# Four neighbouring tokens to a partition: another token order in the load of queries and keys, undone in the copy out of PSUM

## The chip, the cores and the metric

The kernel runs on one core of a Trainium2 chip. The metric is device time in microseconds, the median over runs of the same program. Beside the timed runs one execution was profiled; all rows below come from that one.

## The reference, cut to what matters

Four batch entries, 12 heads, 448 tokens, head size 64. Causal attention is followed by a gated feed-forward part.

```python
scores = (q @ k.transpose(0, 1, 3, 2)) / sqrt(64)         # per batch entry and head, 448 x 448
scores = where(upper triangle, -1e9, scores)
attn   = softmax(scores)                                  # over keys
x      = concat over heads of (attn @ v)                  # 4 x 448 x 768, fp32
h      = relu(x @ w_in); u, v = halves of h               # 768 -> 1024 = 512 + 512
v_n    = layernorm(v) without weights
v_s    = w_spatial @ v_n + b_spatial                      # 448 x 448 over tokens
out    = (u * v_s) @ w_out                                # 512 -> 768
```

The result has to follow the reference with the order of tokens kept everywhere. The change touches the order in which the tokens of `q` and `k` stand on chip before the scores are made.

## The kernel before, in words

The 12 heads of each batch entry are taken two at a time: 24 pairs. The first 10 pairs (`SINGLE`, `TURNED`, together `WIDE`) compute in single precision; the other 14 split every number into two half-precision parts, turn them with transposing transfers, and are not touched by the change.

For a single-precision pair the steps are these. `load` (line 691) issues four transfers on SyncE's queue at line 699: `q` and `k`, two heads each, 112 KB apiece, 40 transfers over the ten pairs. The destination `qk` has 112 partitions; in each lie eight rows of 64 numbers, four chunks of tokens with the two heads side by side. Token `112 c + p` goes to partition `p`, chunk `c`. `qk_turn` (from line 716) makes four TensorE transposes of 112 x 128 for `q` and four for `k` (line 733), each into its 112 columns of one PSUM bank, and copies the bank's 448 columns into the SBUF tile `qkT`: on ScalarE at line 754 or on VectorE at line 756. There are 20 such copies. Then `wide` (line 883) multiplies (matrix products at line 903), takes row maxima on VectorE (928), exponentials on ScalarE (938), scales the rows, transposes them (976), copies them out (1000, 1002) and multiplies by `v` (1208).

Everything is planned ahead: `plan.add` lists some 2,500 operations with an estimated cost, a table `ORDER` sets the sequence in which they are issued, a string `WHERE` sets the engine of those that may run on several. Each engine then works down its own queue in that sequence and waits only where an operand is not there. While the core would otherwise be waiting at the start, TensorE runs short filler products (line 687); how many and where is settled when the program is built. The keys that `plan.add` is given are for the planner; the waits in the program come from the tiles that an instruction reads and writes.

SyncE issues all transfers. A transfer waits for the eighth one before it, since eight semaphores go round.

Of the kernel before, what the change touches and what calls it, by code (L numbers as in the profile page):

```python
# [18 lines left out]
WIDE_PE = 856, 848, 902  # L19
# [278 lines left out]
def kernel(  # L298
# [12 lines left out]
    B, H, S, D = q.shape  # L311
# [4 lines left out]
    CP = 112  # L316
    NU = S // 64
    NCH = S // CP
# [11 lines left out]
    plan = Plan()  # L330
# [10 lines left out]
    def at(buf):  # L341
        return phys[buf.kind][buf.slot]
# [4 lines left out]
    ident = const.tile([128, 128], F32, name="ident")  # L347
# [45 lines left out]
    def q32(t):  # L393
        return t.bitcast(F32)[:, 0:2 * S].rearrange("p (c r) -> p c r", r=128)

    def flat32(t):
        return t.bitcast(F32)[:, 0:S]

    def k32(t):
        return t.bitcast(F32)[:, 2 * S:3 * S]  # L400
# [34 lines left out]
    def c_dve(n, aps=0):  # L435
        return 68 + n / 0.96 + 62 * aps

    def c_act(n, src="S", extra=0):
        return (51 if src == "P" else 93) + n / 1.2 + 93 * extra
# [20 lines left out]
    def const_key(name, sub=0):  # L460
        return ((name,), sub)

    def dma(fn, reads, writes, cost, gate=()):

        plan.add({"SP": cost[0]}, fn, list(reads) + list(gate), writes, move=cost)
# [225 lines left out]
    def load(p):  # L691
        b, i = divmod(p, NP)
        h0 = 2 * i
        s = st[p] = {"qk": Buf("qk")}
        for n, src in enumerate((q, k)):
            if WHOLE[p]:
                for h in range(2):
                    dma(
                        lambda e, n=n, src=src, h=h: nc.sync.dma_start(
                            out=at(s["qk"])[:, n, h:2 * NCH:2], in_=src[b, h0 + h].rearrange("(c p) d -> p c d", p=CP)  # L700
                        ),
                        [], [(s["qk"], (n, h))], LOAD["qk1"],
                    )
                continue
            dma(
                lambda e, n=n, src=src: nc.sync.dma_start(
                    out=at(s["qk"])[:, n], in_=src[b, h0:h0 + 2].rearrange("h (c p) d -> p (h c) d", p=CP)
                ),
                [], [(s["qk"], n)], LOAD["qk2"],
            )  # L710
# [3 lines left out]
    def qk_turn(p):  # L714

        s = st[p]
        t = s["qkT"] = Buf("qkT")
        if not WIDE[p]:

            def clear(e):  # L720

                if not blank.get(at(t).name):
                    nc.gpsimd.memset(q32(at(t)), 0.0)
                    blank[at(t).name] = True

            plan.add({"POOL": 819}, clear, [], [(t, (0, 0)), (t, (0, 1))])
        for n in range(2):
            pt = Buf("ps")

            def turn(e, n=n, pt=pt):  # L730
                src = at(s["qk"])[:, n].rearrange("p (c h) d -> p c (h d)", h=2)
                for c in range(NCH):
                    nc.tensor.transpose(
                        out=at(pt)[:, CP * c:CP * c + CP], in_=src[:, c], identity=ident[:CP, :CP]
                    )

            plan.add(
                {"PE": 386}, turn, [(s["qk"], (n, 0)), (s["qk"], (n, 1)), const_key("ident")],
                [(pt, 0), (t, "room")], cls="T",
            )  # L740
            parts = [(slice(0, 64), 0), (slice(64, 128), 64)] if n == 0 and not WIDE[p] else [(slice(0, 128), None)]
            for i, (rows, c0) in enumerate(parts):

                def copy(e, pt=pt, rows=rows, c0=c0, n=n):
                    src = at(pt)[rows, :S]
                    if c0 is None:
                        dst = k32(at(t)) if n else flat32(at(t))
                        if not n:
                            blank[at(t).name] = False
                    else:  # L750
                        dst = q32(at(t))[rows, :, c0:c0 + 64]
                        src = src.rearrange("p (c r) -> p c r", r=64)
                    if e == "ACT":
                        nc.scalar.activation(out=dst, in_=src, func=AF.Copy)
                    else:
                        nc.vector.tensor_copy(out=dst, in_=src)

                plan.add({"ACT": c_act(S, "P"), "DVE": c_dve(S)}, copy, [(pt, 0)], [(t, (n, i))])
        s["qkT_keys"] = [(t, (0, 0)), (t, (1, 0))] + ([] if WIDE[p] else [(t, (0, 1))])

    def qk_prepare(p):
        if WHOLE[p]:
            qk_turn(p)
            return
# [129 lines left out]
    def wide(p, eb, et):  # L894


        s = st[p]
        banks = [Buf("ps") for _ in GROUPS]
# [9 lines left out]
        def both(g):  # L908
            for i in range(len(GROUPS[g])):
                for h in range(2):  # L910
                    _, q0, n, o0, _ = GROUPS[g + h][i]
                    product(h, q0, n, banks[g + h], o0, 0, 128)

        def last():
            for h in range(2):
                product(h, 384, S, banks[4], 0, 64 * h, 64)
# [2 lines left out]
        whose = [(sums[g // 2], 2 * (g % 2) if g < 2 else g % 2) for g in range(5)]  # L919
        for n, fn in enumerate((lambda e: both(0), lambda e: both(2), lambda e: last())):  # L920
            parts = [(banks[g], u) for g in (2 * n, 2 * n + 1) if g < 5 for u in range(len(GROUPS[g]))]
            plan.add({"PE": WIDE_PE[n]}, fn, s["qkT_keys"], parts + [(eb, "room")], tail=70, cls="R")
        for g, (ps, group) in enumerate(zip(banks, GROUPS)):
            sm, u0 = whose[g]
            for u, (h, q0, n, o0, _) in enumerate(group):
                plan.add(
                    {"DVE": c_dve(n) + 40},
                    lambda e, ps=ps, n=n, u=u0 + u, sm=sm, o0=o0, h=h: nc.vector.tensor_tensor_reduce(  # L928
                        out=at(ps)[:, o0:o0 + n], in0=at(ps)[:, o0:o0 + n],
                        in1=mask[:, 0:n] if h is None else mask2[:, 512 - n:512],  # L930
                        scale=-0.125, scalar=3.0e38, op0=ALU.add, op1=ALU.min, accum_out=at(sm)[:, u:u + 1],
                    ),
                    [const_key("mask" if h is None else "mask2")], [(ps, u), (ps, "t"), (sm, f"m{u0 + u}")], tail=138,
                )
            for u, (_, _, n, o0, c) in enumerate(group):
                plan.add(
                    {"ACT": c_act(n, "P", 2)},
                    lambda e, ps=ps, n=n, u=u0 + u, sm=sm, o0=o0, c=c: nc.scalar.activation(  # L938
                        out=at(eb)[:, 128 * c:128 * c + n], in_=at(ps)[:, o0:o0 + n], func=AF.Exp, scale=-1.0,
                        bias=at(sm)[:, u:u + 1], accum_out=at(sm)[:, 4 + 2 * u:5 + 2 * u],  # L940
                    ),
                    [(sm, f"m{u0 + v}") for v in range(len(group))], [(ps, u), (sm, f"s{u0 + u}"), (eb, c)],
                )
        for n, sm in enumerate(sums):
            m = (4, 2, 1)[n]
            plan.add(
                {"DVE": 70},
                lambda e, m=m, sm=sm: nc.vector.tensor_reduce(
                    out=at(sm)[:, 12:12 + m], in_=at(sm)[:, 4:4 + 2 * m].rearrange("p (u t) -> p u t", t=2),
                    axis=AX.X, op=ALU.add,  # L950
                ),
# [4 lines left out]
                lambda e, m=m, sm=sm: nc.vector.reciprocal(out=at(sm)[:, 12:12 + m], in_=at(sm)[:, 12:12 + m]),  # L956
                [], [(sm, "d")],
            )
        for g, group in enumerate(GROUPS):
            sm, u0 = whose[g]  # L960
# [22 lines left out]
            for i in range(2 if g < 2 else 1):  # L983
# [20 lines left out]
                n = (256, 128)[i] if g < 2 else 128 * cn  # L1004
                plan.add({"ACT": c_act(n, "P"), "DVE": c_dve(n)}, copy, [(pt, 0)], [(et, (g, i))])

    def attend(p):
# [22 lines left out]
        if WIDE[p]:  # L1030
            wide(p, eb, et)
# [404 lines left out]
    tail = [None]  # L1436
# [217 lines left out]

    constants()
    load(0)
    qk_prepare(0)
    prep_in(0)
    load(1)
    v_load(0)  # L1660
    v_prepare(0)
    for p in range(NPAIR):
        if p + 2 < NPAIR:
            load(p + 2)
        if p + 1 < NPAIR:
            if (p + 1) % NP == 0:
                v_load((p + 1) // NP)
            qk_prepare(p + 1)
            v_prepare(p + 1)
        attend(p)  # L1670
        if p == 1:
            prep_in(1)
        if p == 3:
            prep_sp()
        if p == 4:
            prep_out([const_key("wst", 0), const_key("wst", 1)])
        if p % NP == NP - 1:
            ffn(p // NP)
# [35 lines left out]
```

## Time and profile before

| | |
|---|---|
| median of 3 runs | 363.12 us (361.66 to 364.56) |
| the profiled execution's own time | 362.61 us |
| its span, first to last instruction | 360.9 us |
| TensorE busy | 346.5 us, 96% |
| VectorE busy | 281.5 us, 78% |
| ScalarE busy | 267.7 us, 74% |
| transfers | 160,588 packets, 56.18 MB; 154,849 packets under 512 B |

The profiled execution stands 0.51 us under the median. Its span leaves 1.71 us for what lies before the first and behind the last instruction. Busy shares are averages over the whole; attention in single precision lies in the first 110 us, where the three compute engines are loaded otherwise than later.

### The profile page before, as it was taken

Reading aid. Unit: us, or ns where it says so; the run is one execution under the profiler, and the core shown is the slowest. Engines: PE = TensorE matmul, PEld = TensorE weight load, DVE = VectorE, ACT = ScalarE, POOL = GpSimd, SP = SyncE. Lnnn points to the kernel's source line nnn. Section 1 sums busy time; section 2 is a strip of 40 time slices with the busy share of each in tenths; the row PEclk is TensorE's granted clock in tenths of the full one; section 3 lists DMA queues with packets and bytes.
Section 4 is the critical chain, followed back from the end, with each engine's and each line's share of the span. In section 5 each row is a group of like instructions: output and inputs, shape, how many; then the busy total and the mean of one; then the engine's idle time right before and its main releaser. Section 6 shows DMA issues by size and latency. Waiting matters only on the chain. (4 is left out here: it accounts for less than half of the span.)

```text
span 360.9 us, 8078 instructions
## 1 busy us (share of the span) xinstructions
PE 346.5 (96%) x2603; PEld 223.8 (62%) x2603; DVE 281.5 (78%) x1103; ACT 267.7 (74%) x768; POOL 165.4 (46%) x230
## 2 busy tenths in 40 slices
PE   6999999999999898999999999999999999999995
PEld 4576575455555545765555679754765896454694
DVE  4998897998999899877986997887979976242421
ACT  2889999899999898888799887659788774222101
POOL 3421645157654657442467775525576500035400
PEclk9999999999999999999999999999999999999999
DMA  7978988855877899878999998887919978300023
GB/s 167 219 185 220 229 178 202 190 132 123 189 171 174 189 225 174 171 161 169 177 172 214 189 182 188 182 165 129 174 36 175 189 138 160 109 2 0 3 87 88
DMA packets 160588, 56.18 MB, mean 156 GB/s; under 512 B 154849, under 2 KB 156322, under 8 KB 160546
## 3 DMA queue, kind: packets, MB, share of 16 engines
q1 hardware_dynamic: 160546, 55.68, 75.1%
q8 instruction: 20, 0.33, 0.4%
q14 instruction: 22, 0.18, 0.2%
HBM read 26.76 MB, written 5.51 MB: 89 GB/s over the span
## 5 line engine op out<-in xcount | busy, mean ns | idle before, releaser
L1426 PE MATMUL pf<-wi,xT 128*128 128x512 f16 (+1 forms) x360 | 62.5, 338 | 0.0
L1426 PE MATMUL pf<-xT,wi 128*128 128x448 f16 x288 | 60.3, 353 | 0.0
L1426 PE MATMUL pf<-wo,g 128*128 128x384 f32 x288 | 54.8, 341 | 0.0
L1079 ACT ACTIVATE ps<-ps,sm 128x256 f32<-128x256 f32 (+4 forms) x98 | 45.4, 464 | 9.6 <-DVE sm L1067 7.7
L1168 DVE SCALAR_TENSOR_TENSOR e<-ps,sm,e 128x384 f16<-128x384 f32 (+4 forms) x98 | 46.1, 505 | 6.4 <-ACT e L487 6.0
L1426 PEld LDWEIGHTS pf<-wo,g 128*128 128x128 f32 x288 | 49.7, 188 | 1.8 <-issue 1.2
L1067 DVE CUSTOM_DVE_ANT_0 ps<-ps,mask,sc 128x256 f32<-128x256 f32 (+4 forms) x98 | 46.7, 505 | 1.8 <-PE ps L1057 1.1
L487 ACT ACTIVATE e<-ps,sm 128x384 f16<-128x384 f32 (+4 forms) x98 | 44.0, 507 | 3.9 <-DVE sm L1101 1.9
L489 POOL TENSOR_SCALAR e<-e,sm 128x384 f32<-128x384 f32 (+3 forms) x39 | 23.1, 600 | 46.5 <-DVE sm L956 30.4
L1426 PEld LDWEIGHTS <-xT 128*128 128x128 f16 (+1 forms) x360 | 26.7, 103 | 27.3 <-issue 7.5
L1426 PEld LDWEIGHTS <-wi 128*128 128x128 f16 x288 | 27.2, 99 | 26.4 <-issue 3.3
L1426 PE MATMUL pf<-wst,vn 128*128 128x448 f16 (+1 forms) x176 | 36.9, 353 | 0.4 <-ACT u L1571 0.3
L938 ACT ACTIVATE e<-ps,sm 128x128 f32<-128x128 f32 (+3 forms) x70 | 34.4, 507 | 3.2 <-DVE sm L928 2.6
L903 PE MATMUL ps<-qkT 64*128 64x128 f32 (+3 forms) x160 | 27.8, 450 | 0.6 <-ACT wi L487 0.3
L1426 PEld LDWEIGHTS <-vn 128*128 128x128 f16 (+1 forms) x176 | 16.7, 98 | 16.6 <-issue 1.3
L976 PE MATMUL ps<-ident,e 128*128 128x128 f32 x160 | 24.4, 279 | 2.3 <-DVE e L1168 1.2
L928 DVE CUSTOM_DVE_ANT_0 ps<-ps,e 128x128 f32<-128x128 f32 (+2 forms) x60 | 24.3, 441 | 2.6 <-PE ps L903 2.5
L1516 POOL TENSOR_TENSOR ln<-ln,mhalf 128x1 f32<-128x1 f32 (+1 forms) x16 | 9.0, 562 | 37.8 <-DVE ln L1508 35.9
L1057 PE MATMUL ps<-qkT 128*64 128x256 f16 (+4 forms) x196 | 26.0, 284 | 0.0
L1056 PE MATMUL ps<-qkT 128*64 128x256 f16 (+4 forms) x196 | 24.4, 290 | 1.1 <-DVE e L1168 0.6
L489 POOL TENSOR_SCALAR qk<-qk,sc 112x512 f32<-112x512 f32 x17 | 13.2, 778 | 26.6 <-DVE sc L543 11.0
L976 PEld LDWEIGHTS ps<-ident,e 128*128 128x128 f32 x160 | 17.9, 142 | 9.7 <-POOL e L489 2.1
(165 smaller groups left out, 737.3 us busy)
## 6 DMA issues: line engine op xcount, KB each, us to landing
wb<-in_moe_w_in_dram SPq DMA_DIRECT2D x12, 512.0 KB, 5.6
vnat<-in_v_dram SPq DMA_DIRECT2D x24, 192.0 KB, 4.6
out_dram<-o SPq DMA_DIRECT2D x12, 384.0 KB, 3.3
qk<-in_k_dram SPq DMA_DIRECT2D x14, 224.0 KB, 3.8
qk<-in_q_dram SPq DMA_DIRECT2D x14, 224.0 KB, 4.0
o<-in_moe_w_out_dram SPq DMA_DIRECT2D x8, 384.0 KB, 3.4
qk<-in_q_dram SPq DMA_DIRECT2D x20, 112.0 KB, 5.4
qk<-in_k_dram SPq DMA_DIRECT2D x20, 112.0 KB, 4.7
```

Source lines behind the costliest of these rows:

```text
L487: nc.scalar.activation(out=dst, in_=src, func=AF.Copy, scale=scale)
L489: nc.gpsimd.tensor_scalar(out=dst, in0=src, scalar1=scale, scalar2=1.0, op0=ALU.mult, op1=ALU.mult)
L903: nc.tensor.matmul(out=at(bank)[r0:r0 + rn, o0:o0 + n], lhsT=flat32(t)[rows, q0:q0 + rn], rhs=k32(t)[rows, :n], start=True, stop=True, ski ...
L928: lambda e, ps=ps, n=n, u=u0 + u, sm=sm, o0=o0, h=h: nc.vector.tensor_tensor_reduce(out=at(ps)[:, o0:o0 + n], in0=at(ps)[:, o0:o0 + n], in ...
L938: lambda e, ps=ps, n=n, u=u0 + u, sm=sm, o0=o0, c=c: nc.scalar.activation(out=at(eb)[:, 128 * c:128 * c + n], in_=at(ps)[:, o0:o0 + n], fu ...
L976: nc.tensor.transpose(out=at(pt)[:, 128 * i:128 * i + 128], in_=e32(at(eb))[:, c0 + i, :], identity=ident)
L1056: nc.tensor.matmul(out=o, lhsT=w, rhs=qkT[:, 2 + x, :n], start=True, stop=False)
L1057: nc.tensor.matmul(out=o, lhsT=w, rhs=qkT[:, 4 + x, :n], start=False, stop=True)
L1067: lambda e, ps=ps, n=n, u=u, sm=sm, o0=o0, m0=m0: nc.vector.tensor_tensor_reduce(out=at(ps)[:, o0:o0 + n], in0=at(ps)[:, o0:o0 + n], in1=m ...
L1079: nc.scalar.activation(out=dst, in_=src, func=AF.Exp, scale=-1.0, bias=at(sm)[:, u:u + 1], accum_out=at(sm)[:, 4 + 2 * u:5 + 2 * u],)
L1168: lambda e, part=part, src=src, sm=sm, u=u: nc.vector.scalar_tensor_tensor(out=part(1), in0=src(), scalar=at(sm)[:, 12 + u:13 + u], in1=pa ...
L1426: nc.tensor.matmul(out=o, lhsT=a(), rhs=rhs, start=(n0 + n == 0), stop=(n0 + n == len(mms) - 1), skip_group_check=len(out_ap()) > 1,)
```

## The change

A token is put elsewhere in the load and put back in the copy. With the new pattern partition `p` gets the tokens `4 p` to `4 p + 3`, so that a partition's four rows of a head are 1 KB in one piece in memory. In the destination they are still four rows of 256 B, 512 B apart, since the other head's rows lie between. After the transposes, column `112 c + p` of the bank holds token `4 p + c`. The copy reads the bank in that sequence and writes with a step of four numbers (16 B), as 4 runs of 112, so that `qkT` has the tokens in their old order. Nothing after the copy changes.

```diff
@@ load
-  out=at(s["qk"])[:, n, h:2 * NCH:2], in_=src[b, h0 + h].rearrange("(c p) d -> p c d", p=CP)
+  out=at(s["qk"])[:, n, h:2 * NCH:2], in_=src[b, h0 + h].rearrange("(p c) d -> p c d", p=CP)
@@ qk_turn
-  {"PE": 386}, turn, [(s["qk"], (n, 0)), (s["qk"], (n, 1)), const_key("ident")],
+  {"PE": 386}, turn, [(s["qk"], (n, 0)), (s["qk"], (n, 1)), const_key("ident"), const_key("banks")],
@@ qk_turn, copy
-  dst = k32(at(t)) if n else flat32(at(t))
+  dst = (k32(at(t)) if n else flat32(at(t)))[:, 0:S].rearrange("p (r c) -> p c r", c=NCH)
+  src = src.rearrange("p (c r) -> p c r", c=NCH)
@@ wide
-  plan.add({"PE": WIDE_PE[n]}, fn, s["qkT_keys"], parts + [(eb, "room")], tail=70, cls="R")
+  plan.add({"PE": WIDE_PE[n]}, fn, s["qkT_keys"] + [const_key("banks")], parts + [(eb, "room")], tail=70, cls="R")
@@ wide, exponentials
-  [(sm, f"m{u0 + v}") for v in range(len(group))], [(ps, u), (sm, f"s{u0 + u}"), (eb, c)],
+  [(sm, f"m{u0 + v}") for v in range(len(group))] + [const_key("small"), const_key("pads")],
+  [(ps, u), (sm, f"s{u0 + u}"), (eb, c)],
```

The added keys (`banks`, `small`, `pads`) name cells that are set once at the start; they alter the planner's list of dependences. In the built program every engine's sequence, its waits and the filler products are what they were. What differs is the form of the 20 copies and the source pattern of the 40 loads, which is built as 448 rows of 64 where it was 112 x 4 x 64, while the destination stays 112 x 4 x 64. The 40 loads also lose a mark in the built program (`ant_dge_precooked`) that they, the loads of weights and the 128-row loads of `v` carry before, and that the 64-row transfers (line 814, part of line 1649) never had.

In VectorE's queue, at the first copy (`qkT_84` is the turned tile, `ps_72` the bank; the rows around it are cells set to constants):

```order
 L663 MEMSET vnat_88 64x6x64
-L756 COPY qkT_84<-ps_72 128x448
+L757 COPY qkT_84<-ps_72 128x4x112
 L679 MEMSET vn_66 64x256
 L680 MEMSET vn_66 1x512
 L681 MEMSET vn_66 1x512
```

The copy stands at the same place with another shape; the line number is one higher because of the added line.

## Rows read from the trace of the kernel before

**Rows 1.** The page: busy us, share of the span and instructions of each engine.

```profile
PE 346.5 (96%) x2603; PEld 223.8 (62%) x2603; DVE 281.5 (78%) x1103; ACT 267.7 (74%) x768; POOL 165.4 (46%) x230
```

**Rows 2.** Busy time by stretches: stretch, length, engines (instructions), granted clock, DMA share, GB/s.

```profile
0.00:3.80 3.80, 1.04 (x5) 0.47 (x5) 1.79 (x16) 1.28 (x1) 2.88 (x18) 1.00 0.39 89
3.80:10.00 6.20, 6.20 (x37) 4.36 (x37) 3.38 (x12) 1.67 (x5) 0.38 (x5) 1.00 1.01 228
10.00:20.00 10.00, 9.86 (x74) 6.13 (x70) 9.14 (x40) 9.04 (x33) 5.06 (x10) 1.00 1.04 188
20.00:40.00 20.00, 19.32 (x171) 12.78 (x170) 18.51 (x72) 17.68 (x57) 3.96 (x6) 1.00 0.88 223
40.00:60.00 20.00, 19.68 (x147) 12.00 (x147) 18.54 (x65) 19.70 (x61) 13.31 (x17) 1.00 0.95 201
60.00:72.00 12.00, 11.14 (x86) 6.32 (x81) 10.44 (x38) 10.47 (x33) 1.77 (x3) 1.00 0.76 181
72.00:90.00 18.00, 17.57 (x130) 10.52 (x129) 16.71 (x70) 17.63 (x49) 10.93 (x17) 1.00 0.56 131
90.00:110.00 20.00, 19.93 (x145) 10.34 (x143) 19.45 (x84) 19.85 (x58) 11.56 (x15) 1.00 0.76 166
```

**Rows 3.** Timeline of SyncE's queue, first loads: start, us, instruction, count.

```profile
0.79 0.94 SPq L699 DMA_DIRECT2D qk<-in_q_dram  x2
1.77 1.02 SPq L699 DMA_DIRECT2D qk<-in_k_dram  x2
```

**Rows 4.** Line 699 in the first 6 us: from issue to landing.

```profile
DMA to landing us min/median/max: 2.3/2.9/5.4
```

**Rows 5.** Timeline of TensorE, first pair: transposes (L733), score products (L903).

```profile
3.79 0.98 PE L733 MATMUL ps<-ident,qk 112*128 112x112 f32 x4 [1.65 <-POOL e L648]
...
5.24 0.98 PE L733 MATMUL ps<-ident,qk 112*128 112x112 f32 x4
...
6.86 1.37 PE L903 MATMUL ps<-qkT 64*128 64x128 f32 x8
```

**Rows 6.** Timeline of ScalarE: the first copies and the exponential behind them.

```profile
6.26 0.54 ACT L754 ACTIVATE qkT<-ps 128x448 f32<-128x448 f32 x1 [3.64 <-PE ps L733]
8.80 0.54 ACT L754 ACTIVATE qkT<-ps 128x448 f32<-128x448 f32 x1 [2.00 <-DVE sm L928]
9.42 0.37 ACT L938 ACTIVATE e<-ps,sm 128x128 f32<-128x128 f32 x1
```

**Rows 7.** Timeline of SyncE's queue: two unmarked 64-row transfers in a row.

```profile
278.72 1.23 SPq L1649 DMA_DIRECT2D out_dram<-o  x2
```

**Rows 8.** Groups by form: copies out of PSUM on VectorE and ScalarE, count, busy, mean ns.

```profile
L756 DVE COPY qkT<-ps 128x448 f32<-128x448 f32 x9 | 5.5, 616 | 2.6 <-PE ps L733 2.5
L1002 DVE COPY et<-ps 128x128 f32<-128x128 f32 x4 | 1.1, 282 | 0.0
L1002 DVE COPY et<-ps 128x512 f32<-128x512 f32 x1 | 0.7, 680 | 0.0
L754 ACT ACTIVATE qkT<-ps 128x448 f32<-128x448 f32 x11 | 5.9, 549 | 6.2 <-PE ps L733 4.2 <-DVE sm L928 2.0
L1000 ACT ACTIVATE et<-ps 128x512 f32<-128x512 f32 x9 | 5.6, 626 | 0.0
L1000 ACT ACTIVATE et<-ps 128x128 f32<-128x128 f32 x16 | 4.4, 283 | 1.9 <-DVE et L1002 1.8
```

**Rows 9.** Groups by form: a read that takes every second word, and GpSimd's subtraction.

```profile
L1243 DVE TENSOR_SCALAR wa<-wb 128x512 int32<-128x512 int32 x12 | 5.1, 421 | 2.4 <-DMA wb<-in_moe_w_in_dram 2.4
...
L521 POOL TENSOR_TENSOR qks<-qk,qks 112x512 f16<-112x512 f32 x19 | 22.1, 1169 | 3.7 <-DVE qks L485 1.6 <-ACT qks L487 1.5
```

**Rows 10.** Busy time by stretches, with queries and keys only, and with weights among them.

```profile
4.00:5.00 1.00, 1.00 (x7) 0.83 (x6) 0.19 (x1) 0.00 (x0) 0.18 (x3) 1.00 0.98 221
...
8.00:9.00 1.00, 1.00 (x12) 0.81 (x9) 0.55 (x3) 0.20 (x1) 0.00 (x0) 1.00 0.96 287
```

**Rows 11.** The page: packets of all transfers.

```profile
DMA packets 160588, 56.18 MB, mean 156 GB/s; under 512 B 154849, under 2 KB 156322, under 8 KB 160546
```

## The prediction, made before the changed kernel was run

> **What bounds the kernel now.** I begin with the page's busy shares: TensorE is busy 346.5 us of 360.9 [rows 1], more than any other engine. An average does not say what holds it in the part where the change acts, so the second view is busy time by stretches over the first 110 us [rows 2], with all 40 loads and all 20 copies in it. Up to 3.8 us TensorE works 1.04 us; from 3.8 to 10 it is busy throughout, though with the filler products, which are work for show. From 10 to 110 us it idles 2.5 us in all (the stretches' lengths less the busy column, 6 rows), VectorE 7.2 us and ScalarE 5.6 us. So three engines run at 93 to 98% side by side: there is little room for more work on VectorE or ScalarE, but what room there is lies on them and not on TensorE. The granted clock is 1.00 in all of these stretches.
>
> The third view is the timeline of the first 10 us, which is a chain. SyncE issues two loads of `q` in 0.94 us and two of `k` in 1.02 us [rows 3]; a load lands 2.3 to 5.4 us after its issue, 2.9 in the median [rows 4]. TensorE's transposes of `q` start at 3.79 us, those of `k` at 5.24 us, and the first scores at 6.86 us [rows 5]. The fourth load is issued at about 1.77 + 1.02 / 2 = 2.28 us; with the median landing that gives 5.2 us, where the transposes of `k` start. Their copy on ScalarE runs from 6.26 to 6.80 us [rows 6], and the scores follow 0.06 us later. Load four, the transposes, the copy of `k`: none of them has cover at the start. What grows here moves everything that comes after, since the engines behind it are nearly full.
>
> **The loads: issuing.** Same count, same place, same bytes. The 40 issues lose their mark in the built program. No row shows a load of this form without it. The nearest rows are the unmarked 64-row stores: two in a row take 1.23 us [rows 7], against 1.02 us for two marked loads [rows 3]. That is 0.105 us more for each. Lower bound nothing, if the difference belongs to stores; upper bound the whole 0.21 us for each issue, if all of it belonged to one of the two. I take 0.105. At the start four issues lie before the landing of load four: 4 x 0.105 = 0.42 us on the path (0 to 0.84). Behind them the other 36 issues, 3.8 us over 70 us of queue, are covered by the transfers themselves: the 16 DMA engines are busy 1.01 and 1.04 from 3.8 to 20 us [rows 2], and SyncE waits for them. If that cover were gone, a load would be late by some tenths, and tiles of later pairs are asked for ahead of use.
>
> **The loads: moving.** The source is now one piece of 1 KB for a partition, the destination still four runs of 256 B. Most packets are under 512 B already (154,849 of 160,588) [rows 11]; 40 x 448 = 17,920 of them are these loads, if each row is a packet. I take it that a packet stays what the shorter side makes it, 256 B, and that nothing is won: the destination, which I know, has not changed. The other end: with 4 KB weight rows among the traffic the engines moved 287 GB/s in a microsecond where they moved 221 with queries and keys alone [rows 10]. At those rates 112 KB (114,688 B) takes 0.40 us instead of 0.52 us, 0.12 us for each load, 4 x 0.12 = 0.5 us at the start.
>
> [...]
>
> **The copies.** Twenty of them, 9 on VectorE at 616 ns and 11 on ScalarE at 549 ns [rows 8]. Fixed part and part per column come from the neighbouring copies: VectorE (680 - 282) / 384 = 1.04 ns a column, ScalarE (626 - 283) / 384 = 0.89 ns. For 448 columns that is 0.46 and 0.40 us. The reading side is as before, in sequence; the writing side steps 16 B. No row has such a step. The nearest one is VectorE taking every second word, a step of 8 B: 512 of them in 421 ns [rows 9], faster than the contiguous copy of 512 (680 ns). So a step by itself costs nothing there, and the lower end is 0. For the upper end I take the slowest elementwise work in the trace, GpSimd's subtraction at 1169 / 512 = 2.28 ns a column [rows 9]: 448 x (2.28 - 1.04) = 0.56 us more on VectorE, 448 x (2.28 - 0.89) = 0.62 us on ScalarE. I take 0, since the row with a step on the same engine is nearer in kind than another engine's, though it reads and has half the step; the size of the doubt is in the chances.
>
> **Other edits.** The added keys are the planner's alone; sequence, waits and fillers are as before, so they cost nothing and need no cover.
>
> **The sum.** 0.42 us from issuing, 0 from moving, 0 from the copies. Against the profiled execution's own 362.61 us this gives 363.0. That execution stands 0.51 us under the median, 363.12; on the median's scale the forecast is 363.5 us, no change that can be told.
>
> **Rivals.**
>
> *A, the copies get slower by about one column time per column, and it comes through.* Place: each of the 20 copies, with the engine's next instruction right behind it, as the exponential at 9.42 us behind the copy from 8.80 to 9.34 [rows 6]. Price 0.46 us on VectorE, 0.40 on ScalarE. Three of ScalarE's copies lie in the first 12 us (at 6.26, 8.80 and 11.02), where nothing takes it up: 1.2 us. The other 8 on ScalarE add 3.2 us, the 9 on VectorE 4.1 us. If idle time takes them up (5.6 and 7.2 us from 10 to 110 [rows 2]), the time is 363.12 + 0.42 + 1.2 = 364.7 us; if ScalarE's come through whole, 363.12 + 0.42 + 11 x 0.40 = 367.9 us, which is slower. The point that decides: over 1% needs 3.6 - 0.42 = 3.2 us from 11 copies, so 0.29 us on each, with full passage. For it: engines at 93 to 98%. Against it: the step of 8 B that costs nothing, and the idle time.
>
> [...]
>
> *B, the loads move faster.* 0.12 us for each load, so that 0.5 us at the start outweighs the issuing, and VectorE's 2.4 us of waiting for weights (last column of line 1243 [rows 9]) shrinks as the transfer queues empty sooner. Time 363.12 - 0.1 to 363.12 + 0.42 - 0.5 - 2.4, thus 360.6 to 363.0 us. Against it: the destination's runs of 256 B, and that TensorE idles so little from 10 us on.
>
> *C, the change does not do what it says:* the packets remain 256 B and 160,588 in number, and the loads gain nothing. That is part of my forecast, so it needs no other price.
>
> **Chances and range.** Forecast 0.47. A over the 1% bound 0.22; A taken up in part, 364.7 to 366.7 us, 0.16. B 0.10. A start that is worse than counted or something else 0.05. About 1%, 3.6 us, is what a measurement of this kernel can tell from no change. Faster by over 1%, below 359.5: only the far end of B with something unseen, 0.06. Slower by over 1%, above 366.8: 0.24. Within: 0.70. The range goes from 361.0 (most of B inside) to 368.0 (A at full passage); about 1 in 10 lies above it and a little less below. The forecast's own range is 362.5 to 364.7, with issuing from 0 to 0.84 us and a few tenths between runs.
>
> **What would show it.** Right: the copies stay near 616 and 549 ns; packets stay near 160,588; two first loads of `k` take about 1.23 us to issue; the first scores start near 7.3 us; after that TensorE idles as before. Rival A: copies near 1.08 and 0.95 us, with idle time of TensorE before the scores (line 903) and transposes (976) up to 90 us. Rival B: fewer or shorter packets and a DMA share well under 1 from 3.8 to 20 us, with the landing under 2.9 us. I am wrong altogether if TensorE's idle time from 10 to 110 us moves by more than 3 us with copies and loads unchanged, as then something that I have called equal is not.

## The result, and the profile after

| | median | runs | lowest to highest |
|---|---|---|---|
| before | 362.40 us | 6 | 361.35 to 364.56 |
| after | 367.62 us | 6 | 365.86 to 369.15 |

The ratio is 1.0133, with an interval of 1.0100 to 1.0166: slower by 4.8 us (3.6 to 6.0). The forecast, 363.5 us, was 4.1 us too low; the time lies inside the range, at its upper end, and inside what rival A gave (364.7 to 367.9 us). The profiled execution of after took 367.97 us, with a span of 366.2.

The page of after, in the order of [rows 1] and [rows 11]:

```profile
PE 349.6 (95%) x2603; PEld 225.4 (62%) x2603; DVE 284.4 (78%) x1103; ACT 271.4 (74%) x768; POOL 164.9 (45%) x230
...
DMA packets 160588, 56.18 MB, mean 153 GB/s; under 512 B 154849, under 2 KB 156322, under 8 KB 160546
```

Instructions and packets are the same to the last one. VectorE is busy 2.9 us more, ScalarE 3.7 us.

The groups by form that answer to [rows 8] (count, busy us, mean ns of one, idle before them):

```profile
L757 DVE COPY qkT<-ps 128x448 f32<-128x448 f32 x9 | 8.8, 976 | 3.6 <-PE ps L733 3.5
L755 ACT ACTIVATE qkT<-ps 128x448 f32<-128x448 f32 x11 | 10.8, 1002 | 7.8 <-PE ps L733 7.8
L1002 ACT ACTIVATE et<-ps 128x512 f32<-128x512 f32 x9 | 5.7, 631 | 0.0
```

That is the extra work. A copy takes 976 ns on VectorE instead of 616 and 1002 ns on ScalarE instead of 549: 360 and 453 ns more, 0.80 and 1.01 ns for each of 448 columns. The neighbouring copy without a step (631 ns, 626 before) has not changed. In all it is 9 x 0.360 + 11 x 0.453 = 3.2 + 5.0 = 8.2 us of engine time, against 4.8 us in the run time. Two engines share it and run side by side, so the sum is not a time on one path. (The page's busy times grow by less, 6.6 us in all: they count instructions that overlap once, and some of ScalarE's others came out shorter.)

The start, by the timeline. SyncE, which answers to [rows 3]; TensorE, to [rows 5]; ScalarE, to [rows 6] (start, us, instruction, count, idle before it; `...` stands for rows left out):

```profile
0.79 1.41 SPq L699 DMA_DIRECT2D qk<-in_q_dram  x2
2.24 1.29 SPq L699 DMA_DIRECT2D qk<-in_k_dram  x2
```

```profile
4.77 0.98 PE L733 MATMUL ps<-ident,qk 112*128 112x112 f32 x4 [2.62 <-DMA qk<-in_q_dram]
...
6.18 0.95 PE L733 MATMUL ps<-ident,qk 112*128 112x112 f32 x4
...
8.18 1.65 PE L904 MATMUL ps<-qkT 64*128 64x128 f32 x8 [0.41 <-ACT qkT L755]
```

```profile
7.17 0.96 ACT L755 ACTIVATE qkT<-ps 128x448 f32<-128x448 f32 x1 [4.55 <-PE ps L733]
...
10.81 0.97 ACT L755 ACTIVATE qkT<-ps 128x448 f32<-128x448 f32 x1 [2.68 <-PE ps L733]
11.57 0.34 ACT L939 ACTIVATE e<-ps,sm 128x128 f32<-128x128 f32 x1
```

Read from top to bottom: four issues end at 3.53 us instead of 2.79, the transposes start 0.98 us later, the copy of `k` lasts 0.96 us instead of 0.54, and the scores start at 8.18 us instead of 6.86, now with a wait of 0.41 us for that copy. The wait is the copy's growth (0.42 us): here nothing covers it. ScalarE's second copy starts at 10.81 us instead of 8.80, so the lag is 2.0 us by then.

More than the wait comes on top. The same two groups of TensorE's instructions, seven filler products and the next scores, first before, then after:

```profile
8.60 0.93 PE L687 MATMUL pf<-ones 128*128 128x256 f16 x7
9.46 0.92 PE L903 MATMUL ps<-qkT 64*128 64x384 f32 x4
```

```profile
10.56 1.59 PE L687 MATMUL pf<-ones 128*128 128x256 f16 x7
12.09 0.92 PE L904 MATMUL ps<-qkT 64*128 64x384 f32 x4
```

From the first scores to these it is 2.60 us before (6.86 to 9.46) and 3.91 us after (8.18 to 12.09), for the same instructions and with no wait in either. TensorE works at about half of its later pace up to a point that comes later in after: in both traces the transposes start 187 ns apart early on and 96 ns apart later, and the change lies where the trace's record of the granted clock has its first entry, 1.00, at 7.82 us before and at 11.91 us after. Before, TensorE had worked without a pause from 3.79 us up to there; after, from 4.77 us, with the pause of 0.41 us for the copy in between. So the lag of 2.6 us at the second row is 0.9 us of a later start, 0.4 us of waiting and 1.3 us of slower pace. How long the slow pace lasts can be told in all traces of this document (one for each kernel) from the 41 filler products (line 687), which are the same in all: they take 331 to 334 ns on average in the four with slow copies in the first pair (after, `copies_only`, `early_only`, `step_32`), and 308 ns in seven of the nine others, 313 in `step_8` and 320 in `pe_side` (the runs follow below). In the first three of the four the scores wait 0.41 us for the copy. The slow copies and the late change of pace go together, but that the one makes the other is not shown.

Busy time by stretches, to be laid beside [rows 2]:

```profile
3.80:10.00 6.20, 4.83 (x23) 3.47 (x24) 2.19 (x4) 0.96 (x1) 0.38 (x5) 1.00 0.81 191
10.00:20.00 10.00, 9.87 (x60) 5.65 (x60) 7.97 (x39) 7.99 (x29) 3.32 (x7) 1.00 1.15 213
20.00:40.00 20.00, 19.40 (x168) 13.45 (x167) 18.85 (x69) 18.38 (x57) 3.32 (x7) 1.00 0.70 186
40.00:60.00 20.00, 19.12 (x144) 11.44 (x141) 18.40 (x62) 19.18 (x54) 11.64 (x16) 1.00 0.97 201
60.00:72.00 12.00, 11.99 (x85) 6.72 (x85) 11.27 (x40) 11.97 (x40) 4.63 (x6) 1.00 0.76 208
72.00:90.00 18.00, 17.44 (x135) 10.55 (x132) 16.62 (x62) 17.20 (x47) 8.87 (x14) 1.00 0.66 147
90.00:110.00 20.00, 19.68 (x143) 10.72 (x142) 19.37 (x88) 19.83 (x57) 12.36 (x18) 1.00 0.69 146
```

From 10 to 110 us TensorE is idle 2.5 us, VectorE 7.5 and ScalarE 5.4 us; before it was 2.5, 7.2 and 5.6. The sums are nearly the same, but they are not made of the same waits. VectorE's 2.4 us of waiting for weights (line 1243 in [rows 9]) are gone, and so is a wait of TensorE for GpSimd (the one for GpSimd is gone in the trace of `late_only` too, and is there in those of `loads_only`, 1.1 us, and `reversed`, 1.0 us); waits for the slow copies stand there instead. TensorE's wait before (us in total, times, longest), then after VectorE's group by form and TensorE's waits:

```profile
PE ps L976 <- POOL e L489: 0.9, 1, 0.9
```

```profile
L1245 DVE TENSOR_SCALAR wa<-wb 128x512 int32<-128x512 int32 x12 | 5.0, 421 | 0.0
PE ps L904 <- DVE qkT L757: 0.5, 1, 0.5
PE ps L978 <- DVE qkT L757: 0.3, 1, 0.3
```

By stretches, TensorE's idle time falls from 0.86 to 0.01 us between 60 and 72 us and grows from 0.32 to 0.88 us between 40 and 60. So idle time takes up a part of the growth, and the copies make about as much anew. How much is taken up in the median is open, since these waits move from trace to trace: `step_8` (below), with copies almost as before, waits for weights 0.3 us. The lag shows it too. ScalarE's copies on either side of 60 to 71 us, first before, then after:

```profile
59.64 0.57 ACT L754 ACTIVATE qkT<-ps 128x448 f32<-128x448 f32 x1
71.66 0.98 ACT L754 ACTIVATE qkT<-ps 128x448 f32<-128x448 f32 x2
```

```profile
64.13 1.06 ACT L755 ACTIVATE qkT<-ps 128x448 f32<-128x448 f32 x1
75.22 1.81 ACT L755 ACTIVATE qkT<-ps 128x448 f32<-128x448 f32 x2 [0.23 <-PE ps L733]
```

The lag is 4.5 us at the first and 3.6 us at the second. The clock column says 1.00 in every stretch, as before; ahead of the record's first entry that says nothing. The last copy on VectorE starts at 89.6 us instead of 85.2 (first rows of the views below; duration min/median/max, then first and last start).

```profile
L756 DVE COPY qkT<-ps x9: 593/615/625, 4.8 to 85.2; 128x448 f32<-128x448 f32 x9
```

```profile
L757 DVE COPY qkT<-ps x9: 943/980/1000, 5.8 to 89.6; 128x448 f32<-128x448 f32 x9
```

The first row is before, the second after. The lag grows from 1.0 to 4.4 us, though not evenly. On TensorE 1.4 us of it is idle time from 3.8 to 10 us (4.83 us busy instead of 6.20). TensorE also counts 3.1 us more of busy time over the run (349.6 against 346.5) for the same 2,603 instructions; the 1.3 us of slower pace stand there. The largest share of the 3.1 us is in the score products, the same 160 in both, with 27.8 us before (first fence) and 29.2 us after.

```profile
L903 PE MATMUL ps<-qkT 64*128 64x128 f32 (+3 forms) x160 | 27.8, 450 | 0.6 <-ACT wi L487 0.3 <-ACT e L938 0.2
```

```profile
L904 PE MATMUL ps<-qkT 64*128 64x128 f32 (+3 forms) x160 | 29.2, 457 | 1.3 <-DVE qkT L757 0.5 <-ACT qkT L755 0.4 <-ACT e L939 0.2
```

New among the releasers are the two copies, 0.9 us together, both before the score products.

### The profile page after: what moved, and what is told of

The parts are those of the page before. It is cut to its first block, busy times and chain, and to the rows that moved or that the text cites. A ratio compares the mean times of both kernels' runs of the same rounds, so it can differ in the third digit from the quotient of the medians.

```text
span 366.2 us, 8078 instructions
## 1 busy us (share of the span) xinstructions
PE 349.6 (95%) x2603; PEld 225.4 (62%) x2603; DVE 284.4 (78%) x1103; ACT 271.4 (74%) x768; POOL 164.9 (45%) x230
## 2 busy tenths in 40 slices
DMA packets 160588, 56.18 MB, mean 153 GB/s; under 512 B 154849, under 2 KB 156322, under 8 KB 160546
## 5 line engine op out<-in xcount | busy, mean ns | idle before, releaser
L904 PE MATMUL ps<-qkT 64*128 64x128 f32 (+3 forms) x160 | 29.2, 457 | 1.3 <-DVE qkT L757 0.5
```

The source lines that it names most:

```text
L904: nc.tensor.matmul(out=at(bank)[r0:r0 + rn, o0:o0 + n], lhsT=flat32(t)[rows, q0:q0 + rn], rhs=k32(t)[rows, :n], start=True, stop=True, ski ...
```

## The experiments

Three theories stood against each other at first. Theory C, the copies: the growth of all 20 copies makes the time, about equally wherever they stand. Theory S, the start: what counts is what happens before the first scores, issues and first copies; later growth is taken up. Theory Q, the queue: the 36 later loads are issued late too, and tiles arrive late. Then two more questions came: what in the copy costs, and whether the loads could gain anything. All differences in us are the ratio less 1, times the median of before in the same comparison, with the ends of the ratio's interval in brackets.

### Each part alone: `loads_only` and `copies_only`

```diff
@@ loads_only: before, with the new load
-  in_=src[b, h0 + h].rearrange("(c p) d -> p c d", p=CP)
+  in_=src[b, h0 + h].rearrange("(p c) d -> p c d", p=CP)
@@ copies_only: before, with the new copy
-  dst = k32(at(t)) if n else flat32(at(t))
+  dst = (k32(at(t)) if n else flat32(at(t)))[:, 0:S].rearrange("p (r c) -> p c r", c=NCH)
+  src = src.rearrange("p (c r) -> p c r", c=NCH)
```

> The load of four neighbouring tokens alone; the copy out of PSUM is contiguous as before, so the tokens of the ten single-precision pairs stay permuted (the part of the computation that is changed). Theory S (start chain): the loss comes from a late start (fourth load 0.9 us later, first copies 0.4 us longer each) and is passed on whole, while what comes after 14 us is taken up by idle time. Then this alone costs 0.9 to 1.5 us: 363.3 to 363.9 us beside 362.4, first scores near 7.8 us instead of 6.86. Theory C (every copy counts): the loads cost nothing that lasts, 362.4 +- 0.4. Theory Q (the queue of loads: 36 later issues are longer too, and tiles arrive late): 365 to 366.

> The copy with a step of 16 B alone; loads as before, so the tokens are put in a wrong order (the part that is changed). Theory S: 2.5 to 3.5 us more than before, 365 to 366 us, nearly all of it by 25 us on the chip's clock; copies near 0.98 us on VectorE and 1.00 us on ScalarE as in the changed kernel. Theory C: all 11 copies of ScalarE come through, 11 x 0.45 = 5.0 us, 367.4 us, the lag growing evenly up to 86 us. Theory Q: 1 to 1.5 us more, 363.4 to 363.9 us.

`loads_only`: median 362.55 us against 362.49, ratio 1.0002 (0.9976 to 1.0029): +0.1 us (-0.9 to 1.1). `copies_only`: 367.82 us, ratio 1.0156 (1.0112 to 1.0201): +5.7 us (4.1 to 7.3). The groups by form of `copies_only`:

```profile
L757 DVE COPY qkT<-ps 128x448 f32<-128x448 f32 x9 | 8.8, 974 | 2.8 <-PE ps L733 2.7
L755 ACT ACTIVATE qkT<-ps 128x448 f32<-128x448 f32 x11 | 10.8, 1002 | 7.1 <-PE ps L733 7.1
```

The copies alone give the whole slowdown, with 974 and 1002 ns, as in after. Theory C's 5.0 us for them holds; theory S's 2.5 to 3.5 us lies below the interval, and theory Q's 1 to 1.5 us far below it. The loads alone give nothing that can be told, though their issues are as slow as in after (1.41 and 1.29 us for two), so theory S's share for the loads is refuted in its upper part, and theory Q's 365 to 366 us altogether.

### The mark on the loads: `unmarked`

```diff
@@ load: before, with the 40 loads issued without their mark
+  nc.dge_precook = False
   nc.sync.dma_start(...)
+  nc.dge_precook = True
```

> The kernel before with the mark taken from its 40 single-precision loads; token order, copies and everything else as before. If the mark is all that the loads cost (theory S), this is the same as the kernel with the new load alone within 0.5 us, two issues take near 1.29 us instead of 1.02, and the fourth load lands near 5.5 us instead of 4.96. If the contiguous source gains something of its own, this is slower than the new load alone by 0.5 us or more; if it costs something, faster by as much.

Median 363.47 us, ratio 1.0043 (1.0014 to 1.0072): +1.6 us (0.5 to 2.6). Timeline of SyncE in this run:

```profile
0.80 1.43 SPq L701 DMA_DIRECT2D qk<-in_q_dram  x2
2.26 1.30 SPq L701 DMA_DIRECT2D qk<-in_k_dram  x2
```

So the longer issue comes from the lost mark and not from the order of tokens. As to its worth, this run and `loads_only` agree only where their intervals overlap, at 0.5 to 1.1 us. Its median is 0.9 us above that of `loads_only`, more than the 0.5 us that was allowed if the mark were all; a gain from the contiguous source would look like this, but `reversed` (below) has that source with the mark kept and shows none.

### Where a slower copy comes through: `early_only` and `late_only`

```diff
@@ qk_turn, copy: before, with the new copy in some pairs
+  if p < 2:        # early_only; in late_only: if p > 1
+      dst = dst[:, 0:S].rearrange("p (r c) -> p c r", c=NCH)
+      src = src.rearrange("p (c r) -> p c r", c=NCH)
```

> The counterpart: the step of 16 B for the pairs 0 and 1 alone, 4 copies before 12 us (wrong token order there, the part that is changed). Theory S: 2 us or more, by the lag of 2.2 us that the kernel with all copies stepped has at 12 us. Theory C: 4/20 of the whole, 0.8 to 1.5 us. The sum with the kernel of late copies should give the 4.0 to 7.3 us of all twenty.

> Loads as before; the copy with a step of 16 B for the pairs 2 to 9 alone, 16 copies from 17 us on (their tokens are put in a wrong order, the part that is changed). Theory S (only the copies at the start come through, later ones are taken up by idle time): 0 to 1 us more than before. Theory C (every copy counts alike): 16/20 of the 4.0 to 7.3 us that all twenty cost, 3.2 to 5.8 us.

The copies by form, of `early_only` and then of `late_only` (the means mix slow and unchanged copies):

```profile
L757 ACT ACTIVATE qkT<-ps 128x448 f32<-128x448 f32 x11 | 7.2, 663 | 8.9 <-PE ps L733 8.9
L759 DVE COPY qkT<-ps 128x448 f32<-128x448 f32 x9 | 5.9, 653 | 3.6 <-PE ps L733 3.6
```

```profile
L757 ACT ACTIVATE qkT<-ps 128x448 f32<-128x448 f32 x11 | 9.5, 885 | 5.6 <-PE ps L733 4.0 <-DVE sm L931 1.6
L759 DVE COPY qkT<-ps 128x448 f32<-128x448 f32 x9 | 8.5, 944 | 2.8 <-PE ps L733 2.7
```

| | growth of the copies | time | interval |
|---|---|---|---|
| `early_only` | 11 x 114 + 9 x 37 ns = 1.6 us | 364.22, +2.4 us | 1.4 to 3.3 |
| `late_only` | 11 x 336 + 9 x 328 ns = 6.6 us | 365.09, +3.3 us | 2.3 to 4.3 |
| `copies_only` | 11 x 453 + 9 x 358 ns = 8.2 us | 367.82, +5.7 us | 4.1 to 7.3 |

The two parts add up to the whole, in growth and in time. The growth in the first two pairs comes through in full (1.6 us lies in the interval), of the growth in the other eight about half does (2.3 to 4.3 of 6.6). Theory S falls on `late_only`, for which it had 0 to 1 us. Theory C had 3.2 to 5.8 us there, which fits, and 0.8 to 1.5 us for `early_only`, which is less than was measured, though the intervals touch. What fits best is between: the start passes everything on, the full stretch behind it about half.

Two things keep this from being a law of passage. In the trace of `early_only` the start has the pause of 0.41 us and the slow pace behind it, as in after (four transposes from 9.85 us on take 1.01 us, seven filler products from 10.65 us on 1.70 us; before, 0.60 and 0.93), so its 2.4 us are not the growth of four copies alone. And by time the half cannot be told from ScalarE's growth whole and VectorE's not at all: that would be 3.7 us for `late_only` and 5.0 us for `copies_only`, both inside, and 1.3 us for `early_only`, just below. The traces speak against the second reading, since TensorE waits for VectorE's copies too: 0.5 and 0.3 us in after, 0.4 and 0.3 us in `late_only`.

### What in the copy costs: `step_8`, `step_32`, `pairs`

```diff
@@ qk_turn, copy: before, and in the new copy another pattern of the same 448 columns
   dst = (k32(at(t)) if n else flat32(at(t)))[:, 0:S].rearrange(...)
   step_8:  dst "p (r c) -> p c r", c=2         src "p (c r) -> p c r", c=2
   step_32: dst "p (r c) -> p c r", c=8         src "p (c r) -> p c r", c=8
   pairs:   dst "p (r c t) -> p c r t", c=4, t=2   src "p (c r t) -> p c r t", c=4, t=2
```

Writes go every second word, every eighth word, or two neighbouring words at a time with 32 B from pair to pair.

> Loads as before; all twenty copies write with a step of two numbers, 8 B, as two runs of 224 (tokens in a wrong order, the part that is changed). [...] If any step in writing costs, copies at 0.98 and 1.00 us and 366 us or more. [...]

> Loads as before; the copies write with a step of eight numbers, 32 B, as 8 runs of 56 (wrong token order, the part that is changed). Read from the durations alone. [...]

> Loads as before; the copies write two neighbouring numbers and then step 32 B, 4 runs of 56 pairs (wrong token order, the part that is changed). [...] If the innermost run being short is what costs, more than 1 us.

The groups by form, in that order:

```profile
L757 DVE COPY qkT<-ps 128x448 f32<-128x448 f32 x9 | 5.6, 617 | 3.0 <-PE ps L733 2.9
L755 ACT ACTIVATE qkT<-ps 128x448 f32<-128x448 f32 x11 | 6.3, 587 | 7.0 <-PE ps L733 6.9
```

```profile
L757 DVE COPY qkT<-ps 128x448 f32<-128x448 f32 x9 | 8.7, 970 | 2.0 <-PE ps L733 1.9
L755 ACT ACTIVATE qkT<-ps 128x448 f32<-128x448 f32 x11 | 10.9, 1011 | 7.4 <-PE ps L733 7.4
```

```profile
L757 DVE COPY qkT<-ps 128x448 f32<-128x448 f32 x9 | 5.5, 617 | 2.6 <-PE ps L733 2.5
L755 ACT ACTIVATE qkT<-ps 128x448 f32<-128x448 f32 x11 | 6.4, 590 | 6.3 <-PE ps L733 4.0 <-DVE sm L929 2.3
```

A step of 8 B is free on VectorE (617 ns against 616) and costs ScalarE 38 ns (587 against 549); 16 B costs 360 and 453 ns; 32 B costs the same within 3%, 354 and 462 ns. With 32 B but two words side by side it is free again on VectorE (617 ns) and costs ScalarE 41 ns (590). So it is neither the split pattern nor the size of the largest step. In the two slow forms every word lies 16 B or more from the one written before it; in the two fast ones each has, next to it in the sequence of writing, a word that is 4 or 8 B away. Where between 8 and 16 B the cost begins, and why, these runs do not show. In time `step_8` is 362.07 us, ratio 0.9994 (0.9971 to 1.0018); `step_32` and `pairs` had one run each, 367.18 and 361.10 us against 362.23, which fits.

### The step on the other side: `read_side` and `pe_side`

Both have the new load and put the tokens back elsewhere: `read_side` reads the bank with a step of 112 words and writes in sequence; in `pe_side` the transposes write the bank with a step of 16 B and the copy is the old one.

```diff
@@ read_side: after, with
-  dst = (k32(at(t)) if n else flat32(at(t)))[:, 0:S].rearrange("p (r c) -> p c r", c=NCH)
-  src = src.rearrange("p (c r) -> p c r", c=NCH)
+  dst = (k32(at(t)) if n else flat32(at(t)))[:, 0:S].rearrange("p (r c) -> p r c", c=NCH)
+  src = src.rearrange("p (c r) -> p r c", c=NCH)
@@ pe_side: after, with the old copy and
-  out=at(pt)[:, CP * c:CP * c + CP], in_=src[:, c], identity=ident[:CP, :CP]
+  out=at(pt)[:, c:S:NCH], in_=src[:, c], identity=ident[:CP, :CP]
```

> The changed kernel with the order restored on the other side of the copy: it reads the PSUM bank with a step of 448 B (four numbers, one from each chunk) and writes contiguously; the whole computation is as in the reference. If the step costs on the writing side only: copies near 0.62 us (VectorE) and 0.55 us (ScalarE), and the time is that of the new load alone, 363.3 to 363.9 us. If a step costs on the reading side as well: copies at 0.95 us or more and 367 us or more.

> The changed load; the order is restored a step earlier, by the transposes, which write the PSUM bank with a step of 16 B, and the copy is contiguous on both sides. The whole computation is as in the reference. If PSUM takes such writes like contiguous ones: transposes at 0.26 us in the median, as before. If a step in PSUM costs TensorE: 0.35 us or more each, 80 of them, 7 us or more of TensorE's time. Copies 0.62 and 0.55 us either way.

Groups by form of `read_side`; then, by the tile `qk`, the transposes of `pe_side` (duration ns min/median/max, first and last start):

```profile
L757 DVE COPY qkT<-ps 128x448 f32<-128x448 f32 x9 | 5.5, 616 | 3.8 <-PE ps L733 3.7
L755 ACT ACTIVATE qkT<-ps 128x448 f32<-128x448 f32 x11 | 5.9, 548 | 7.2 <-PE ps L733 5.3 <-DVE sm L929 1.7
```

```profile
L733 PE MATMUL ps<-ident,qk x80: 257/260/447, 4.9 to 85.7; 112*128 112x112 f32 x80
```

`read_side`: 363.39 us, ratio 1.0023 (0.9993 to 1.0054). The same rearrangement with the step on the reading side costs the copies nothing. `pe_side`, one run: 364.07 us against 362.23, within what runs of one kernel differ by; its transposes take 260 ns in the median (259 before), so these stepped writes of TensorE cost nothing in this one trace.

### Whether neighbouring rows move faster with the mark kept: `reversed`

```diff
@@ load and copy: read_side, with the four tokens of a partition last first
+  in_=src[b, h0 + h].rearrange("(p c) d -> p c d", p=CP)[:, ::-1]
+  src = src.rearrange("p (c r) -> p r c", c=NCH)[:, :, ::-1]
```

> Four neighbouring tokens to a partition, the last one first, so that the source pattern stays 112 x 4 x 64 and the loads keep their mark; the copy restores the order on its reading side. The whole computation is as in the reference. If the mark is what the loads' issues cost: two issues take 1.02 us again and the first scores start near 6.9 us. If neighbouring rows move faster by themselves, landing under 2.9 us in the median of the first 6 us and a time under 362.5 us by up to 1.5; if not, the time of the kernel before within 0.5 us.

Timeline of SyncE, and line 699 in the first 6 us from issue to landing:

```profile
0.80 0.95 SPq L699 DMA_DIRECT2D qk<-in_q_dram  x2
1.78 1.02 SPq L699 DMA_DIRECT2D qk<-in_k_dram  x2
```

```profile
DMA to landing us min/median/max: 2.3/3.0/6.2
```

The issue is as short as before, the four rows of a partition are neighbours, and they land in 3.0 us (2.9 in [rows 4]). Time 363.17 us, ratio 1.0021 (0.9998 to 1.0044). Nothing is won by the neighbourhood; no variant with several runs beats the kernel before, and the one run of `pairs`, 361.10 us, lies among the runs of that kernel.

## Why the prediction came out as it did

The time lies inside the range, but not by the forecast, which had 0.42 us of growth where 4.8 us came. The range reached up to 368.0 us for the sake of rival A, to which the text gave 0.38 in all; that the time fell inside is this rival's doing.

**What bounds the kernel: right, with two gaps.** Three engines at 93 to 98%, with no cover at the start, fit a slowdown of 4.8 us from 8.2 us of growth on two engines. The first gap is TensorE's pace. The text read a clock of 1.00 in all stretches, but up to 7.8 us the transposes started 187 ns apart and not 96, and a later change of pace, worth 1.3 us in the trace of after, is no term of the sum. The second is the idle time that might take the growth up. VectorE's 2.4 us of waiting for weights did go, as did 0.9 us of TensorE's, while waits for the copies came in their place; the text had only the sums of idle time to go by, and they hardly move.

**Issuing: right in kind, too small, and worth little.** Two marked issues take 0.94 and 1.02 us, two unmarked 1.41 and 1.29, so 0.235 and 0.135 us more for each instead of 0.105, and 0.74 us before load four instead of 0.42 (inside the 0 to 0.84). In the run time it is -0.9 to 1.1 us by `loads_only`. The start also moves by itself: with marked loads the first transposes began at 3.79 us ([rows 5]), 3.99 (`copies_only`), 4.25 (`reversed`) and even 4.85 (`early_only`); without the mark at 4.77 (after), 4.88 (`loads_only`) and 4.76 (`unmarked`). So how much of the 0.98 us that the two profiles show at the start is the loads' doing is open.

**Moving: right.** The packets are 160,588 as before, and `reversed` shows no faster landing. Rival B has nothing for it; the prediction's estimate of what larger packets could win was not put to the test, as the packets did not grow.

**The copies: this step failed.** "I take 0, since the row with a step on the same engine is nearer in kind than another engine's ..." Measured: 0.36 us on VectorE and 0.45 us on ScalarE for each copy, and 5.7 us (4.1 to 7.3) of run time for all twenty by `copies_only`. The row with the step of 8 B could not tell. It differs in side and in size (and reads SBUF, where the copy reads PSUM), and the size is enough to mislead: `step_8` shows that 8 B is almost free on the writing side too (617 and 587 ns), so that its cheapness says nothing of 16 B. Reading SBUF with a step of 16 B was not tried.

**Rival A: right in place and price.** It said 0.46 and 0.40 us for a copy; 0.36 and 0.45 were measured, above its deciding point of 0.29 us on ScalarE's eleven. Its two ends, 364.7 (taken up) and 367.9 us (ScalarE's whole, VectorE's not), held the result. The upper end is a growth of 4.8 us over the median of 363.12 that it was reckoned from, just what was measured over 362.40. That this sum agrees is in part luck: it has 0.42 us of issuing that `loads_only` does not show, nothing for the slower pace, and nothing for VectorE's copies, for which TensorE does wait.

**The signs.** Named for A were copies near 1.08 and 0.95 us (976 and 1002 ns) and TensorE waiting before the scores (0.9 us, for both copies) and the transposes of line 976 (0.3 us). Both are seen; the sum of idle time up to 110 us does not show them, as other waits went. Of the signs for the forecast, the first loads of `k` came near theirs (1.29 us for 1.23), while the first scores were due near 7.3 us and came at 8.18.

## What to carry to other kernels

Writing 448 words to SBUF with 16 or 32 B from each word to the next cost a copy 0.35 to 0.46 us here, so put a reordering on the reading side of a copy out of PSUM, or keep two neighbours together: the first was free here (616 and 548 ns), the second all but free (617 and 590 ns). A row of the trace with half the step is no evidence for the whole one: 8 B cost at most 0.04 us. And growth is worth what its place lets through: here all of it or more in the first pairs, where a pause of TensorE went along with a late change of its pace, and about half in the full stretch. Equal sums of idle time do not say that nothing was taken up or lost: compare the waits one by one, and the start of the same instruction in both traces.

## What the runs showed of the hardware that was not expected

- From 16 to 32 B the cost does not grow: both steps cost the same (976 and 970 ns on VectorE, 1002 and 1011 ns on ScalarE), and ScalarE pays more for a word (1.01 ns against 0.80).
- ScalarE pays a little even with a step of 8 B or with pairs of neighbours: 587 and 590 ns against 549, where VectorE pays nothing (617 against 616).
- Reading PSUM with a step of 448 B costs neither engine anything (616 and 548 ns), nor does TensorE's writing it with 16 B (260 ns).
- A load without its mark takes longer to issue, and no longer to land: 1.41 us instead of 0.94 for the first two, with a median of 3.0 us from issue to landing in the first 6 us of after (2.9 before).
- TensorE ran at about half of its later pace from its first work up to 7.8 us before and up to 11.9 us after (a transpose every 187 ns instead of 96), although the clock column shows 1.00 there; the later change of pace cost 1.3 us, three times the wait of 0.41 us that came ahead of it.
